# State input of an S5 and gated-GLU kernel: the last 64 features of re and im as half-row products beside those of gate and up

## The chip, the core and the metric

The kernel runs on one core of a Trainium2 chip. The metric is device time in microseconds of one execution. Clocks are granted to TensorE by a throttle; the profile gives the granted clock (here 0.997 of full speed over the span).

## What is computed

Cut to what matters, for x of 2048 tokens by D = 448 features, 448 states and F = 1792:

```
xn = layernorm(x)
Bu = xn @ B_bar^T             # complex: re and im, 448 states each
h[t] = Lam_bar * h[t-1] + Bu[t]     # scan over 2048 tokens, per state
s  = 2 * real(h @ C^T) + xn * Dskip
g  = silu((sigmoid(xn @ w_gate) * (xn @ w_up)) @ w_down)
out = x + s * g
```

The kernel multiplies with B alone; the factor of B_bar is worked into C. The complex scan is turned into two real ones by rotating re and im with tables of cosine and sine.

## The kernel before, in words

Tokens are cut into four chunks of 512. In a chunk all products have features on the partitions and 512 tokens as columns (`xnT`, the normalized input, transposed). 448 features are three whole tiles of 128 rows and one of 64. Names that the steps below use:

- *Gate and up* (`gu_mm`, L589; 14 feature tiles `ft` per chunk): each is three whole products (L603) and one of 64 rows (L597). The 64-row weights of gate lie in rows 0 to 63 of `wt`, those of up in rows 64 to 127, and row tile 3 of `xnT` holds the last 64 features twice (for chunk 0 the second copy is in a fifth tile of its own), so that the two half-row products use the two halves of the rows of TensorE. An even `ft` ends with its halves and an odd `ft` begins with them, so four halves stand together once in two tiles. ScalarE takes the sigmoid of gate (L616) and copies up (L620); VectorE multiplies them to `hF` (L625), one tile later.
- *State input* (`emit_bu`, L454; sets (chunk, pt)): for pt 0 to 2, re and im of 128 states, four products each (L460), the fourth with 64 rows of zeros; pt 3 is one group of four, with the last 64 states of re and of im side by side. ScalarE copies the result to `bus` (L471, L532). Its twelve or so VectorE pieces (rotate L477 to L484, scan L490, rotate back L504 to L512; for pt 3 L538 to L574, with half exchanges by DMA in between, `swap_halves`) go to a list.
- *The planner* (`fill`, L687): pieces are taken from that list, in order, when a running account of TensorE time against VectorE time has room. `unread` counts sets whose `bus` is still to be read. A new set is taken behind an odd `ft` only if fewer than two are unread (L825).
- *Down and output*: `emit_down` (L638, 14 products a token tile of 128, two readings by ScalarE, the product `g_t` L650 on VectorE) and `emit_y` (L658: six products with `h` of pt 0 to 2 L663, one with `h` of pt 3 L665, four with the diagonal of Dskip L669), then `emit_fin` on VectorE (L676, L678) and the store (L679). The outputs of a chunk come in the next chunk, from `ft` 9 on, once all four `h` of it are placed.
- *Banks*: PSUM's eight banks are two for gate (tag g), two for up (u), and four accumulators (acc) for down and output. The state input takes acc in chunk 0, and g and u later.
- *Order*: each engine runs its instructions in the order of the program. All loads, transposes and stores after the first rows are on SP's queue. B comes in rows (`raw`, L146) and is turned by eight DMA transposes into `bT` (`emit_b`, L273, L279). The columns past 448 are zero. The normalized input of chunks 1 to 3 is turned the same way (L257), when ScalarE or VectorE has written it and its second copy of the last 64 features (`ln_twice`). The input of chunk 2, and C with its turns (L163, L167, factors `ct` L428, L429), are loaded in chunk 0.
- *POOL* makes the tables' mirrored halves (`emit_mirror`, L411), a few small vectors and the carries of the scan.

Of the kernel before, what the change touches and what calls it, by code (L numbers as in the profile page):

```python
# [17 lines left out]
D = 448  # L18
F = 1792
P = 128  # L20
TC = 512
# [3 lines left out]
KT = 4  # L25
FT = F // P
DP = KT * P
# [20 lines left out]
def bcast_mid(ap: bass.AP, n: int) -> bass.AP:  # L48
    return ap.unsqueeze(1).to_broadcast((ap.shape[0], n, ap.shape[1]))
# [14 lines left out]
def kernel(  # L64
# [18 lines left out]
    pe, act, dve, pool, sync = nc.tensor, nc.scalar, nc.vector, nc.gpsimd, nc.sync  # L83
# [16 lines left out]
    xnT = [w.tile([P, KT + 1, TC], BF16, name=f"xnT{c}") for c in range(3)]  # L100
# [6 lines left out]
    bT = w.tile([P, KT, NPK], BF16, name="bT")  # L107
# [7 lines left out]
    def load_rows(eng, t, mat, f0, f1):  # L115
        eng.dma_start(out=t[:, 0:3, f0:f1], in_=mat[0:384, f0:f1].rearrange("(kt p) f -> p kt f", p=P))
        eng.dma_start(out=t[0:64, 3, f0:f1], in_=mat[384:448, f0:f1])

    def load_w(eng, f0, f1):
        for t, mat, p0 in ((wg, B_w_gate, 0), (wu, B_w_up, 64)):  # L120
            eng.dma_start(out=t[:, :, f0:f1], in_=mat[0:384, f0:f1].rearrange("(kt p) f -> p kt f", p=P))
            eng.dma_start(out=wt[p0:p0 + 64, f0:f1], in_=mat[384:448, f0:f1])
# [16 lines left out]
    raw = {}  # L139

    def load_x(c):
        if c == 3:
            x_t.append(w.tile([P, TPC, D], BF16, name="x3", tag="tc_re"))
        sync.dma_start(out=x_t[c][:], in_=x_src[:, c * TPC:(c + 1) * TPC, :])

    for nm, mat in (("b_re", A_B_re), ("b_im", A_B_im)):  # L146
        raw[nm] = w.tile([P, KT, DP], BF16, name=nm, tag="raw" + nm[1:])
        dve.memset(raw[nm][:, :, D:DP], 0.0)
        load_rows(sync, raw[nm], mat, 0, D)
    load_w(sync, 512, 1024)  # L150
    load_x(1)

# [116 lines left out]
    def ln_out(j, tp, copy):  # L269
        copy(out=xnT[0][:, :, j * P:(j + 1) * P], in_=tp[:])  # L270


    def emit_b(cc, pt):  # L273
        n = P if pt < 3 else 64
        if cc == 0:
            p0 = pt * P
        else:
            p0 = D if pt == 3 else 512 + pt * P
        sync.dma_start_transpose(out=bT[:, :, p0:p0 + n], in_=raw[("b_re", "b_im")[cc]][0:n, pt, :])  # L279

    def bu_cols(pt, cc):
        if pt == 3:
            return 384, 512
        return (pt * P, (pt + 1) * P) if cc == 0 else (512 + pt * P, 512 + (pt + 1) * P)
# [5 lines left out]
    def col(name, n=KT):  # L290
        return w.tile([P, n], FP32, name=name)
# [19 lines left out]
    def emit_steps():  # L311
        kq, nf, anf = col("kq", 2 * KT), col("nf", 2 * KT), col("anf", 2 * KT)
        tu = col("tu", 2 * KT)
        pool.tensor_copy(out=tu[:, 0:KT], in_=K["turn"][:])
        pool.tensor_single_scalar(out=tu[:, KT:2 * KT], in_=K["theta"][:], scalar=float(TC) / TWO_PI, op=ALU.mult)
        pool.tensor_single_scalar(out=kq[:], in_=tu[:], scalar=MAGIC, op=ALU.add)
        pool.tensor_single_scalar(out=kq[:], in_=kq[:], scalar=-MAGIC, op=ALU.add)
        pool.tensor_tensor(out=nf[:], in0=kq[:], in1=tu[:], op=ALU.subtract)
        dve.tensor_single_scalar(out=anf[:].bitcast(I32), in_=nf[:].bitcast(I32), scalar=0x7FFFFFFF,
                                 op=ALU.bitwise_and)  # L320
        sn, cs = col("sn", 2 * KT), col("cs", 2 * KT)
        act.activation(sn[:], nf[:], ACT.Sin, scale=-SIN_SCALE)
        act.activation(cs[:], anf[:], ACT.Sin, scale=-TWO_PI, bias=hpi[:])
        K.update(sn=sn, cs=cs)
# [118 lines left out]
    unread = [0]  # L443

    def bank(spare, tag, name):
        if spare:
            return ps.tile([P, TC], FP32, name=name, tag="acc", bufs=4)
        return ps.tile([P, TC], FP32, name=name, tag=tag)
# [2 lines left out]
        sync.dma_start(out=o[0:64, :], in_=i[64:128, :])  # L451
        sync.dma_start(out=o[64:128, :], in_=i[0:64, :])

    def emit_bu(c, pt):  # L454
        unread[0] += 1

        def mms(pst, cc):
            lo, hi = bu_cols(pt, cc)
            for kt in range(KT):
                pe.matmul(pst[:], lhsT=bT[:, kt, lo:hi], rhs=xnT[c][:, kt, :],  # L460
                                 start=(kt == 0), stop=(kt == KT - 1))

        rb = K["r"][:, pt:pt + 1].to_broadcast((P, TC))
        mul, add = ALU.mult, ALU.add
# [1 line left out]
        if pt < 3:  # L466
            bus = sp.tile([P, 2, TC], BF16, name="bus", bufs=3)
            for cc in range(2):
                pst = bank(c == 0, ("g", "u")[cc], "bu")
                mms(pst, cc)  # L470
                act.copy(out=bus[:, cc, :], in_=pst[:])  # L471
            cosb = bcast_mid(cosT[:, pt, :], 2)
            sv = spm[:, pt, :, :]

# [51 lines left out]
            for f in (p3, p4, p5):  # L526
                later(0.69, f)
        else:
            pst = bank(c == 0, "g", "bu3")
            mms(pst, 0)  # L530
            bus = sp.tile([P, TC], BF16, name="bus3", tag="bus", bufs=3)
            act.copy(out=bus[:], in_=pst[:])  # L532
            bsw = sp.tile([P, TC], BF16, name="bsw3", bufs=1)
            swap_halves(bsw, bus)

# [50 lines left out]
        if due:  # L586
            due.pop(0)()

    def gu_mm(c, ft, gt, ut, n0=0, n1=TC):  # L589


        f0, f1 = ft * P, (ft + 1) * P
        first = ft % 2 == 1

        def halves():
            for t, p0 in ((gt, 0), (ut, 64)):
                pe.matmul(t[:, n0:n1], lhsT=wt[p0:p0 + 64, f0:f1], rhs=xnT[c][p0:p0 + 64, KT if c == 0 and p0 else 3, n0:n1],  # L597
                          start=first, stop=not first)

        def wholes():  # L600
            for t, wm in ((gt, wg), (ut, wu)):
                for kt in range(3):
                    pe.matmul(t[:, n0:n1], lhsT=wm[:, kt, f0:f1], rhs=xnT[c][:, kt, n0:n1],  # L603
                              start=(not first and kt == 0), stop=(first and kt == 2))

        for part in ((halves, wholes) if first else (wholes, halves)):
            part()

    def emit_gu(c, ft):
        gt, ut = bank(False, "g", "g_ps"), bank(False, "u", "u_ps")  # L610
        gu_mm(c, ft, gt, ut)
        gu_out(c, ft, gt, fp.tile([P, TC], BF16, name="ub"), ut)

    def gu_out(c, ft, gt, ub, ut=None):
        sig = fp.tile([P, TC], BF16, name="sig")
        act.activation(sig[:], gt[:], ACT.Sigmoid)  # L616
        if ut is up_copy:
            up_copy(ft)
        elif ut is not None:
            act.copy(out=ub[:], in_=ut[:])  # L620
        emit_mul()

        def mul():
            h = fp.tile([P, TC], BF16, name="hF", bufs=23)
            dve.tensor_tensor(out=h[:], in0=sig[:], in1=ub[:], op=ALU.mult)  # L625
            hF[c, ft] = h

        due.append(mul)
# [4 lines left out]
    def emit_gate():  # L633
        if due_g:
            due_g.pop(0)()
# [51 lines left out]
    def fill(pe, own):  # L687
        clock[0] += 1
        room[0] = min(room[0] + pe - own, 2.0)
        while pieces and room[0] > 0.0 and clock[0] >= popped[0] + pieces[0][2]:  # L690
            cost, fn, _ = pieces.pop(0)
            popped[0] = clock[0]
            room[0] -= cost
            fn()
# [70 lines left out]
    for pt in range(2, KT):  # L765
        emit_frac(pt)
        emit_sin(pt)
        emit_cos(pt)
    emit_steps()
    for pt in range(KT):  # L770
        emit_neg(pt)
        emit_mirror(pt)
# [36 lines left out]
    at(1, 8, 0.0, lambda: load_x(3))  # L809
    ln_plan(2)  # L810
    ln_plan(3)
    bu_q, out_q = [], []
    room[0] = -2.0
    for c in range(NCH):
        bu_q.extend((c, pt) for pt in range(KT))
        for ft in range(4 if c == 0 else 0, FT):
            emit_gu(c, ft)
            emit_gate()
            for cost, f in beside.pop((c, ft), ()):
                room[0] -= cost  # L820
                f()
            fill(1.62 if c < NCH - 1 or ft < 9 else 2.2, 0.42)
            if ft % 2 == 0:
                continue
            if (4 if c == 0 else 0) < ft < FT - 1 and bu_q and unread[0] < 2:  # L825
                emit_bu(*bu_q.pop(0))
                popped[0] = clock[0]
                fill(1.7, 0.0)
            if c == 0:
                continue  # L830
            if ft < 8:
                emit_down(c - 1, ft // 2)
                fill(2.66, 0.39)
                if ft == 7:
                    out_q.extend((c - 1, j) for j in range(TPC))
            if c == NCH - 1 and ft == FT - 1:
                emit_mul()
            for _ in range(2 if ft == 11 else 1):
                if not (out_q and ft >= 8 and all((out_q[0][0], pt) in hs for pt in range(KT))):
                    break  # L840
                emit_y(*out_q[0])
                emit_fin(*out_q.pop(0))
                fill(1.53, 1.01)
    flush()
    c = NCH - 1
# [38 lines left out]
```

## Time and profile before

| | us |
|---|---|
| three runs, median (lowest to highest) | 197.91 (197.82 to 328.5) |
| the profiled execution | 197.33 |
| its span, first to last instruction | 195.5 |
| TensorE busy (matmul), weight load | 188.8, 90.7 |
| VectorE, ScalarE, POOL busy | 156.8, 111.0, 42.3 |

By stage, each stretch in us from the start of the span:

| stretch | length | TensorE | VectorE | ScalarE |
|---|---|---|---|---|
| start, to 15.5 | 15.5 | 14.10 | 11.06 | 12.63 |
| chunk 0, to 38.0 | 22.5 | 22.24 | 20.86 | 15.83 |
| chunk 1, to 82.7 | 44.7 | 44.30 | 37.67 | 29.35 |
| chunk 2, to 129.3 | 46.6 | 46.17 | 41.18 | 26.20 |
| chunk 3, to 174.7 | 45.4 | 45.19 | 38.07 | 23.09 |
| last outputs, to 195.5 | 20.8 | 16.83 | 7.92 | 3.87 |

How to read the profile: a line of a timeline gives start, duration, engine, source line, operation, output and inputs, shape and count; instructions that follow each other are merged. In brackets stands the idle time before it and what ended that. A group's line gives busy time, mean ns of one, and idle time before it. A matmul's duration is the time from its issue to its modelled end; matmuls that follow each other overlap, so the distance between two starts is what one takes of TensorE's time.

### The profile page before, as it was taken

How to read it: one execution, taken by the hardware profiler on the slowest of the kernel's cores; microseconds unless marked ns; L12 is line 12 of the kernel's file. 1: busy time of each engine (PE TensorE's matmuls, PEld its weight loads, DVE VectorE, ACT ScalarE, POOL GpSimd, SP SyncE). 2: the span in 40 equal slices, each digit the busy share in tenths (PEclk: the TensorE clock that was granted, in tenths of full speed). 3: DMA queues.
4: the chain of work that ended last, by engine and by line, in shares of the span. 5: the costliest groups of instructions: out<-in, count | busy, mean ns of one | idle time of the engine just before them, and what ended most of it. 6: DMA issues, size and time to landing. Idle time of an engine off the chain costs nothing.

```text
span 195.5 us, 3111 instructions
## 1 busy us (share of the span) xinstructions
PE 188.8 (97%) x1069; PEld 90.7 (46%) x1084; DVE 156.8 (80%) x322; ACT 111.0 (57%) x214; POOL 42.3 (22%) x93
## 2 busy tenths in 40 slices
PE   7999999999999999999999999999999999999991
PEld 6874434344444445444444444444444444545561
DVE  4898799948969799999984999999419999994223
ACT  4998666665488856455474586335736644241130
POOL 3535598950302200010321031002100000000000
PEclk9999999999999999999999999999999999999998
DMA  5997994995300302511001001430100010020100
GB/s 153 302 296 140 257 107 86 358 271 100 74 0 15 106 0 64 108 34 27 0 5 29 0 0 38 96 97 0 27 0 3 0 27 2 25 76 23 47 25 23
DMA packets 27593, 14.87 MB, mean 76 GB/s; under 512 B 16309, under 2 KB 27577, under 8 KB 27577
## 3 DMA queue, kind: packets, MB, share of 16 engines
q1 hardware_dynamic: 27568, 14.67, 32.5%
q8 instruction: 8, 0.13, 0.3%
q14 instruction: 9, 0.07, 0.2%
q10 hardware_dynamic: 8, 0.00, 0.0%
HBM read 8.38 MB, written 1.84 MB: 52 GB/s over the span
## 4 chain that ended last, share of the span: by engine, by line
PE 91%; DMA 3%; DVE 2%; issue 1%; ACT 1%; POOL 0%; ACTq 0%; DVEq 0%
PE d_ps L641 22%; PE g_ps L603 20%; PE u_ps L603 18%; PE bu L460 12%; PE y_ps L663 8%; PE g_ps L597 8%; PE y_ps L669 1%; DMA x<-in_A_x_dram 1%; PE y_ps L665 1%; DMA xnT<-xn 1%; DVE stats L207 1%; DVE xnT L270 0%; ACT junk L221 0%; DVE sg L676 0%; POOL sd L234 0%
## 5 line engine op out<-in xcount | busy, mean ns | idle before, releaser
L616 ACT ACTIVATE sig<-g_ps 128x512 bf16<-128x512 f32 x56 | 33.2, 599 | 34.9 <-PE u_ps L597 32.2
L603 PE MATMUL g_ps<-xnT,wg 128*128 128x512 bf16 (+1 forms) x169 | 45.5, 366 | 1.1 <-issue 0.3
L603 PE MATMUL u_ps<-xnT,wu 128*128 128x512 bf16 (+1 forms) x176 | 45.4, 365 | 0.2
L641 PE MATMUL d_ps<-wd,hF 128*128 128x448 bf16 x224 | 45.0, 353 | 0.0
L620 ACT CAST ub<-u_ps 128x512 bf16<-128x512 f32 x52 | 30.3, 583 | 1.7
L641 PEld LDWEIGHTS <-hF 128*128 128x128 bf16 x224 | 21.6, 98 | 20.4
L644 ACT ACTIVATE sigd<-d_ps 128x448 bf16<-128x448 f32 x16 | 8.7, 543 | 33.8 <-PE d_ps L641 33.8
L460 PE MATMUL bu<-xnT,bT 128*128 128x512 bf16 x112 | 26.8, 379 | 0.0
L603 PEld LDWEIGHTS <-wu 128*128 128x128 bf16 x180 | 17.5, 98 | 18.8 <-DMA wu<-in_B_w_up_dram 0.2
L625 DVE TENSOR_TENSOR hF<-sig,ub 128x512 bf16<-128x512 bf16 x56 | 23.4, 420 | 2.3 <-ACT ub L620 2.3
L603 PEld LDWEIGHTS <-wg 128*128 128x128 bf16 x180 | 14.5, 98 | 22.3 <-issue 12.3
L490 DVE TENSOR_TENSOR_SCAN wv<-r_col,st,ta 128x512 bf16<-128x512 f32 x18 | 22.5, 1271 | 0.3
L650 DVE TENSOR_TENSOR g_t<-zb,sigd 128x448 bf16<-128x448 bf16 x16 | 6.2, 390 | 19.1 <-ACT zb L646 19.1
L663 PE MATMUL y_ps<-ct,h 128*128 128x448 bf16 (+1 forms) x102 | 21.0, 342 | 0.0
L597 PE MATMUL g_ps<-xnT,wt 64*128 64x512 bf16 (+1 forms) x60 | 17.2, 367 | 0.0
L597 PE MATMUL u_ps<-xnT,wt 64*128 64x512 bf16 (+1 forms) x60 | 17.2, 367 | 0.0
L460 PEld LDWEIGHTS <-bT 128*128 128x128 bf16 x112 | 11.0, 98 | 13.2
L497 POOL TENSOR_TENSOR tq<-wv,smT 128x2 f32<-128x2 bf16 x9 | 4.1, 450 | 57.6 <-DVE wv L490 57.6
L471 ACT CAST bus<-bu 128x512 bf16<-128x512 f32 x24 | 13.8, 586 | 4.5 <-PE bu L460 4.5
L663 PEld LDWEIGHTS <-h 128*128 128x128 bf16 x102 | 9.7, 98 | 8.3
L207 DVE BATCH_NORM_STATS2 stats<-x 128x6 f32<-128x448 bf16 x14 | 8.6, 617 | 5.8 <-DMA x<-in_A_x_dram 5.8
L676 DVE TENSOR_TENSOR sg<-y_ps,g_t 128x448 bf16<-128x448 f32 (+1 forms) x17 | 10.0, 586 | 0.7 <-PE y_ps L669 0.3
(130 smaller groups left out, 213.6 us busy)
## 6 DMA issues: line engine op xcount, KB each, us to landing
out_dram<-o_t SPq DMA_DIRECT2D x15, 112.0 KB, 1.7
wd<-in_B_w_down_dram SPq DMA_DIRECT2D x1, 1568.0 KB, 7.7
x<-in_A_x_dram SPq DMA_DIRECT2D x3, 448.0 KB, 3.5
wg<-in_B_w_gate_dram SPq DMA_DIRECT2D x2, 384.0 KB, 5.3
wu<-in_B_w_up_dram SPq DMA_DIRECT2D x2, 384.0 KB
wg<-in_B_w_gate_dram SPq DMA_DIRECT2D x1, 576.0 KB, 4.4
wu<-in_B_w_up_dram SPq DMA_DIRECT2D x1, 576.0 KB, 6.6
bsw<-bus SPq DMA_DIRECT2D x8, 64.0 KB, 2.0
```

The costliest lines, as they stand in the source:

```text
L207: dve.bn_stats(out=stats[:], in_=x_t[t // TPC][:, t % TPC, :])
L460: pe.matmul(pst[:], lhsT=bT[:, kt, lo:hi], rhs=xnT[c][:, kt, :], start=(kt == 0), stop=(kt == KT - 1))
L471: act.copy(out=bus[:, cc, :], in_=pst[:])
L490: dve.tensor_tensor_scan(out=T["wv"][:, cc, :], data0=rb, data1=T["ta"][:, cc, :], initial=(0.0 if c == 0 else st[pt][:, cc, :]), op0=mul, ...
L597: pe.matmul(t[:, n0:n1], lhsT=wt[p0:p0 + 64, f0:f1], rhs=xnT[c][p0:p0 + 64, KT if c == 0 and p0 else 3, n0:n1], start=first, stop=not first)
L603: pe.matmul(t[:, n0:n1], lhsT=wm[:, kt, f0:f1], rhs=xnT[c][:, kt, n0:n1], start=(not first and kt == 0), stop=(first and kt == 2))
L616: act.activation(sig[:], gt[:], ACT.Sigmoid)
L620: act.copy(out=ub[:], in_=ut[:])
L625: dve.tensor_tensor(out=h[:], in0=sig[:], in1=ub[:], op=ALU.mult)
L641: pe.matmul(d[:], lhsT=hF[c, ft][:, j * P:(j + 1) * P], rhs=wd[:, ft, :], start=(ft == 0), stop=(ft == FT - 1))
L663: pe.matmul(y[:, d0:d1], lhsT=hs[c, pt][:, cc, sl], rhs=ct[:, 2 * pt + cc, d0:d1], start=(pt == 0 and cc == 0), stop=False)
L676: dve.tensor_tensor(out=sg[:, d0:d1], in0=ys[c, j][:, d0:d1], in1=gs[c, j][:, d0:d1], op=ALU.mult)
```

## The change

For the state input, the last 64 features are taken out of the group of four and become one product of 64 rows for re (rows 0 to 63) and one for im (rows 64 to 127), or re alone for pt 3. They are issued at the start of the group (start=True), right behind the two half-row products of an odd `ft` of gate and up and before its whole products; the three whole products of the state input stay behind that `ft`. So that rows 64 to 127 of `bT` tile 3 hold the last 64 features of im, POOL copies them into the columns past 448 of `b_im` before the transposes; only `b_re` is still filled with zeros there. The banks are always accumulators. Whether a set is taken is decided before the gate and up products of the odd `ft`, and no longer behind them and their `fill`; the allowance of `fill` behind a set goes from 1.7 to 1.5.

```diff
-        dve.memset(raw[nm][:, :, D:DP], 0.0)
         load_rows(sync, raw[nm], mat, 0, D)
+    dve.memset(raw["b_re"][:, :, D:DP], 0.0)
...
+    def emit_b_twice():
+        t = raw["b_im"]
+        pool.tensor_copy(out=t[:, 0:3, D:DP], in_=t[:, 0:3, 384:D])
+        pool.tensor_copy(out=t[0:64, 3, D:DP], in_=t[0:64, 3, 384:D])
...
+    def bu_halves(c, pt):
+        pst = []
+        for cc in range(2 if pt < 3 else 1):
+            p0, (lo, hi) = 64 * cc, bu_cols(pt, cc)
+            t = bank(True, None, "bu")
+            pe.matmul(t[:], lhsT=bT[p0:p0 + 64, 3, lo:hi], rhs=xnT[c][p0:p0 + 64, KT if c == 0 and p0 else 3, :],
+                      start=True, stop=False)
+            pst.append(t)
+        return pst
...
-            for kt in range(KT):
-                pe.matmul(pst[:], lhsT=bT[:, kt, lo:hi], rhs=xnT[c][:, kt, :],
-                                 start=(kt == 0), stop=(kt == KT - 1))
+            for kt in range(3):
+                pe.matmul(pst[:], lhsT=bT[:, kt, lo:hi], rhs=xnT[c][:, kt, :], start=False, stop=(kt == 2))
...
-                pst = bank(c == 0, ("g", "u")[cc], "bu")
-                mms(pst, cc)
-                act.copy(out=bus[:, cc, :], in_=pst[:])
+                mms(pst[cc], cc)
+                act.copy(out=bus[:, cc, :], in_=pst[cc][:])
...
-        for part in ((halves, wholes) if first else (wholes, halves)):
-            part()
+        if not first:
+            wholes()
+        halves()
+        if beside_halves is not None:
+            beside_halves()
+        if first:
+            wholes()
...
     emit_steps()
+    emit_b_twice()
...
         for ft in range(4 if c == 0 else 0, FT):
-            emit_gu(c, ft)
+            bu = None
+            if ft % 2 == 1 and (4 if c == 0 else 0) < ft < FT - 1 and bu_q and unread[0] < 2:
+                bu = bu_q.pop(0)
+                emit_gu(c, ft, lambda: bu_pst.append(bu_halves(*bu)))
+            else:
+                emit_gu(c, ft)
...
-            if (4 if c == 0 else 0) < ft < FT - 1 and bu_q and unread[0] < 2:
-                emit_bu(*bu_q.pop(0))
+            if bu is not None:
+                emit_bu(*bu, bu_pst.pop())
                 popped[0] = clock[0]
-                fill(1.7, 0.0)
+                fill(1.5, 0.0)
```

More of the change, by code (lines that the diff above doesn't have):

```diff
@@ L452, in swap_halves, with emit_bu @@
         sync.dma_start(out=o[64:128, :], in_=i[0:64, :])
-    def emit_bu(c, pt):
+    def bu_halves(c, pt):
[7 more added lines that the diff above has]
+        return pst
+    def emit_bu(c, pt, pst):
         unread[0] += 1
@@ L528, in emit_bu @@
         else:
-            pst = bank(c == 0, "g", "bu3")
-            mms(pst, 0)
+            mms(pst[0], 0)
             bus = sp.tile([P, TC], BF16, name="bus3", tag="bus", bufs=3)
-            act.copy(out=bus[:], in_=pst[:])
+            act.copy(out=bus[:], in_=pst[0][:])
             bsw = sp.tile([P, TC], BF16, name="bsw3", bufs=1)
@@ L587, in emit_mul, with gu_mm @@
             due.pop(0)()
-    def gu_mm(c, ft, gt, ut, n0=0, n1=TC):
+    def gu_mm(c, ft, gt, ut, n0=0, n1=TC, beside_halves=None):
         f0, f1 = ft * P, (ft + 1) * P
@@ L604, in wholes, with emit_gu @@
                               start=(not first and kt == 0), stop=(first and kt == 2))
-        for part in ((halves, wholes) if first else (wholes, halves)):
-            part()
-    def emit_gu(c, ft):
+        if not first:
[5 more added lines that the diff above has]
+            wholes()
+    def emit_gu(c, ft, beside_halves=None):
         gt, ut = bank(False, "g", "g_ps"), bank(False, "u", "u_ps")
-        gu_mm(c, ft, gt, ut)
+        gu_mm(c, ft, gt, ut, beside_halves=beside_halves)
         gu_out(c, ft, gt, fp.tile([P, TC], BF16, name="ub"), ut)
@@ L811 @@
     ln_plan(3)
-    bu_q, out_q = [], []
+    bu_q, out_q, bu_pst = [], [], []
     room[0] = -2.0
```

## The prediction

> **What bounds the kernel now.** I read the page's busy shares and chain of waits, then the groups by line, then the timeline of TensorE around one of the steps that change, and last the timelines of VectorE and ScalarE where a step moves.
>
> ```profile
> PE 188.8 (97%) x1069; PEld 90.7 (46%) x1084; DVE 156.8 (80%) x322; ACT 111.0 (57%) x214; POOL 42.3 (22%) x93
> PE 91%; DMA 3%; DVE 2%; issue 1%; ACT 1%; POOL 0%; ACTq 0%; DVEq 0%
> L460 PE MATMUL bu<-xnT,bT 128*128 128x512 bf16 x112 | 26.8, 379 | 0.0
> ```
>
> TensorE is busy 97% of the span and is 91% of the chain; the state input (`bu`) never waits (idle 0.0). So a TensorE instruction taken away is time taken away, as long as nothing that TensorE waits for becomes late. The 379 ns of one instruction is no price: they overlap. The price is the distance between starts:
>
> ```profile
> 16.40 0.81 PE L603 MATMUL u_ps<-xnT,wu 128*128 128x512 bf16 x3
> 17.14 0.39 PE L597 MATMUL g_ps<-xnT,wt 64*128 64x512 bf16 x1
> 17.14 0.39 PE L597 MATMUL u_ps<-xnT,wt 64*128 64x512 bf16 x1
> 17.37 0.38 PE L597 MATMUL g_ps<-xnT,wt 64*128 64x512 bf16 x1
> 17.37 0.38 PE L597 MATMUL u_ps<-xnT,wt 64*128 64x512 bf16 x1
> 17.68 0.82 PE L603 MATMUL g_ps<-xnT,wg 128*128 128x512 bf16 x3
> 18.34 0.81 PE L603 MATMUL u_ps<-xnT,wu 128*128 128x512 bf16 x3
> 18.98 1.89 PE L460 MATMUL bu<-xnT,bT 128*128 128x512 bf16 x8
> 20.71 0.59 PE L603 MATMUL g_ps<-xnT,wg 128*128 128x512 bf16 x2
> ```
>
> Eight state products take 20.71 - 18.98 = 1.73 us, 0.216 each. A half-row product of gate and one of up start together, and the next pair 0.223 later (0.22 to 0.23 by the rounded rows): two for the price of one. Going in costs 0.09 (16.40 + 3 x 0.216 = 17.05, not 17.14), coming out 0.09 (17.37 + 0.22 = 17.59, not 17.68).
>
> **The change, part by part.**
>
> *Products.* For pt 0 to 2, two whole products of 0.216 become one pair of halves of 0.223: 0.209 saved, for 4 chunks x 3 = 12 sets: **-2.51 us**. The pair joins a section that exists, so the 0.09 in and out aren't paid again. For pt 3, one whole becomes a half with no partner: 4 x (0.223 - 0.216) = +0.03. All of it lies on TensorE's path.
>
> The Trainium skill, "TensorEngine Tiling (Array Packing)", section Performance Considerations, speaks against a gain: tiling makes TensorE faster but not the emptying of PSUM, which may then bound. If it held here the 2.51 would be lost whole. The rows say otherwise for this kernel: ScalarE, which empties these banks, is busy 57%.
>
> *Slots.* Whether a set is taken is now decided before the gate and up products of its slot, when fewer of the earlier set's VectorE pieces have been placed. By the order of the built program seven sets move one odd feature tile later or more: (chunk, pt) (0,3) from behind tile 11 of chunk 0 to tile 1 of chunk 1; (1,0) from 1 to 3, (1,1) from 7 to 9, (1,2) from 9 to 11 of chunk 1; (2,1), (2,2), (2,3) by two tiles each. TensorE's work is the same, so moving costs only through lateness. Two places matter.
>
> *First place, gain: the end of chunk 2.*
>
> ```profile
> 126.81 2.44 DMA xnT<-xn
> 128.75 0.36 PE L669 MATMUL y_ps<-diag,xnT 128*128 128x128 bf16 x4
> 129.30 0.82 PE L603 MATMUL g_ps<-xnT,wg 128*128 128x512 bf16 x3 [0.19 <-DMA xnT<-xn]
> ```
>
> Chunk 3 starts late because its transposed input lands at 129.25. The last diagonal product starts at 128.92, and elsewhere the next product follows 0.03 later, so 0.35 is lost. The transposes are issued after the norm at tile 10. Set (2,3), 3 x 0.216 + 0.22 = 0.87, now lies between tile 10 and chunk 3, so TensorE comes 0.87 later relative to the transposes: **-0.35**. Its two swap transfers also leave SP's queue ahead of the transposes; they had been issued by 119.1, before the norm was ready, so that is worth nothing. Bounds: 0 to -0.35; I take -0.35, as 0.87 covers it twice.
>
> *Second place, loss: the first output of chunk 0.* It needs `h` of pt 3, whose pieces now stand further back on VectorE.
>
> ```profile
> 44.50 0.63 DVE L207 BATCH_NORM_STATS2 stats<-x 128x6 f32<-128x448 bf16 x1 [3.12 <-DMA x<-in_A_x_dram]
> 60.48 1.23 DVE L550 TENSOR_TENSOR_SCAN wv<-r_col,ta 128x512 bf16<-128x512 f32 x1
> 67.21 0.42 DVE L574 TENSOR_TENSOR h<-tcs,td 128x512 bf16<-128x512 bf16 x1
> 71.04 0.35 PE L665 MATMUL y_ps<-ct,h 128*128 128x448 bf16 x1
> ```
>
> Now `h` ends at 67.63, needed at 71.04. VectorE waits at 44.50 for the load of chunk 2, which is not moved, so I count from there. Newly between 44.50 and the scan (steps from start to start): three pieces of earlier sets (0.72 + 0.61 + 0.60), two `hF` (0.67), one `g_t` (0.30), three `ct` (1.80), two small vectors (0.29): 5.0. VectorE idles 1.55 before `ct` at 55.63, because ScalarE's factor comes late; the new work ahead of it fills that. So the scan ends at 61.6 + 5.0 - 1.55 = 65.1. Then the swap through SP: in chunk 3 its reader waits from the scan's end at 173.66 to 176.35, 2.7. So the reader starts at 67.8, `h` ends 0.9 later, at 68.7. TensorE wants it at 71.04, less set (1,2), now behind it (1.73), less five savings (1.05): 68.3. **+0.45** on the path. Bounds: 0 (VectorE 0.45 earlier) and +2.0 (the idle 1.55 not filled). I take 0.45: `ct` is reached at 56.05 by the count, its factor was ready at 55.6.
>
> *Waits of the new pairs.* Six whole products stand behind each, so a late operand or bank stops TensorE. Tightest: set (0,0) at 17.59 needs two `acc` banks whose sigmoids end by
>
> ```profile
> 15.07 2.06 ACT L616 ACTIVATE sig<-g_ps 128x512 bf16<-128x512 f32 x4
> ```
>
> 17.13, and the `b_im` transpose, landed at 16.93 by the trace's landing records; set (0,2), at about 27.1 (22.33 + 4.96, a slot's length, + 0.22 - 0.42), needs one landed at 26.7. Both have 0.4 to spare: 0, bounds 0 and +0.4 (if the transposes slip by 0.8). For the later sets I followed the banks through the built order: each was emptied several us earlier, most by ScalarE, some by the output product on VectorE. Gate and up no longer lend banks; they show no idle for it now, so nothing is gained.
>
> *Two copies on POOL, one memset less on VectorE.* The nearest rows are POOL's copies of 128x255 at 0.40, so 0.8 at most for both. The data has landed at 11.2 (7.04 + 4.2); POOL is idle from 11.34 to 13.20 and only the mirror at 10.94 slips to 12.0, its reader starting at 25.3. SP issues the first `b_im` transpose at 12.95, behind that of `b_re`: 0.9 to spare. Nothing on the path; without that cover at most 0.8 on the transposes, of which 0.4 would reach TensorE. The memset (0.17 at 0.96) lay in VectorE's wait for x: 0.
>
> *The two turns of C* are no longer behind the first swap on SP, but their own load lands at 41.4 and they started at 41.49: 0.
>
> *The tail.* `h` of pt 3, chunk 3, ends at 177.23 and is needed at 178.45, 1.2 spare; one `hF` (0.33) now precedes its scan, and VectorE follows TensorE again from 153.3. 0.9 spare: 0.
>
> **Sum:** -2.51 + 0.03 - 0.35 + 0.45 = -2.38. The profiled execution took 197.33 (span 195.5 and 1.8 around it), so 194.95; the median of the three runs is 197.91, 0.58 above. A measured median of **195.5** follows, 1.2% less. About 2% either way is what a measurement of this kernel can tell from no change.
>
> **Rivals.**
>
> *A. The output waits longer (197.1).* If VectorE's 1.55 idle stays, the wait is 2.0 in place of 0.45. For it: ScalarE's factor waits for a transposed C whose last piece landed at 54.7, unmoved by any speed. Against: 2.0 us of VectorE's work moved ahead of that wait.
>
> *B. The halves don't overlap (198.0).* If re and im ran one after the other, a pair would cost 0.43 and save nothing: -0.35 + 0.45. Against: all 52 pairs in the trace start 2 to 5 ns apart, with the same row halves and other banks.
>
> *C. Slower: `h` of pt 3 very late (198 to 202).* The place is the first output of chunk 0; the price is one us for each us of lateness, and it decides from 2.9 of wait (2.51 + 0.35), that is a scan ending after 67.5 in place of 65.1. For it: VectorE is 80% busy, and the swap and a dozen queued pieces follow. Against: it needs 2.4 us that the count from 44.50 doesn't contain.
>
> **How the numbers follow.** The forecast, 194.8 to 196.4 (wait 0 to 1.2): 0.70. A, to 197.7: 0.14. B: 0.05. C: 0.07, 0.03 of it above 201.9. A gain past what the sum holds: 0.04, 0.03 of it over 2%. Forecast and A make the range, 194.8 to 197.7. Faster by over 2% (below 194.0): 0.03; slower by over 2% (above 201.9): 0.03; within: 0.94.
>
> **What would show it.** Right: `bu` with 12 x 6 + 4 x 3 whole and 28 half products, three pairs 0.22 apart in a section; no DMA wait before chunk 3; VectorE's scan of pt 3 near 65 and an idle of TensorE near 68 to 69 of about 0.5 before L665's successor. Wrong: pairs 0.43 apart (B), an idle of 2 us there (A) or 3 (C), or idle ahead of the first product of a new pair, which would be a bank or a transpose that I called early.

## The result and the profile after

The changed kernel takes 194.61 us in the median of four runs (194.35 to 194.86). The kernel before, run beside it, takes 197.87 (197.70 to 197.91, and one slow run of 328.5 that the ratio leaves out). The ratio is 0.9838, with a 95% interval of 0.9816 to 0.986. In a second measurement it was 194.48 against 197.44: 0.9852 (0.9839 to 0.9866). So the change brings 1.5 to 1.6%. The prediction said 195.5, with 194.8 as its lower end: the sign and the main mechanism were right, the gain was larger than forecast, and the range was too high by 0.2 us.

The profiled execution took 194.83 (span 193.1), against 197.33 (195.5) before. First the busy shares of the page, then the share of the span by engine on the chain that ended last, then the state input's groups (out<-in, shape, count | busy us, mean ns of one | idle before them), all of the changed kernel:

```profile
PE 186.9 (97%) x1084; PEld 88.8 (46%) x1084; DVE 157.2 (81%) x321; ACT 111.7 (58%) x214; POOL 45.1 (23%) x95
...
PE 90%; DMA 3%; ACT 2%; DVE 2%; SPq 1%; issue 1%; ACTq 0%; DVEq 0%
```

```profile
L477 PE MATMUL bu<-xnT,bT 128*128 128x512 bf16 x84 | 20.7, 379 | 0.0
L466 PE MATMUL bu<-xnT,bT 64*128 64x512 bf16 x28 | 6.1, 376 | 0.0
```

There are 84 whole and 28 half products, neither with idle time before it. TensorE is still busy 97% of a span that is 2.5 shorter (195.53 to 193.06). Its timeline around one set of the changed kernel (start, duration, engine, line, output and inputs, shape, count):

```profile
27.15 0.39 PE L611 MATMUL g_ps<-xnT,wt 64*128 64x512 bf16 x1
27.15 0.39 PE L611 MATMUL u_ps<-xnT,wt 64*128 64x512 bf16 x1
27.38 0.38 PE L611 MATMUL g_ps<-xnT,wt 64*128 64x512 bf16 x1
27.38 0.38 PE L611 MATMUL u_ps<-xnT,wt 64*128 64x512 bf16 x1
27.59 0.38 PE L466 MATMUL bu<-xnT,bT 64*128 64x512 bf16 x2
27.91 0.82 PE L617 MATMUL g_ps<-xnT,wg 128*128 128x512 bf16 x3
28.56 0.81 PE L617 MATMUL u_ps<-xnT,wu 128*128 128x512 bf16 x3
29.21 1.03 PE L477 MATMUL bu<-xnT,bT 128*128 128x512 bf16 x4
```

The two half products of the set are one entry ("x2", 0.38 together). The first begins 0.216 after the first of the pair of gate and up, by the raw starts (0.212 after the second), and the way out to 27.91 takes 0.31, as it did without them.

To place the rest I use one measure for all kernels below. The *steady part* runs from the start of the first 512-wide product of gate (`ft` 4, chunk 0) to the start of the last matmul. From it I take off the distances between starts that are longer than elsewhere: between the last diagonal product (the one with the diagonal of Dskip) of a chunk's outputs and the next product of gate (0.028 elsewhere), which is the *wait for the turned input*, and before the product with `h` of pt 3 (0.189 elsewhere), which is the *wait for h*. The *start stall* is the same ahead of the first 512-wide product (0.109 elsewhere). What is left of the steady part is products.

| kernel (one profile each) | start stall | input waits, chunk 2 + 3 | wait for h | steady | products alone | ratio of times to before (95%) |
|---|---|---|---|---|---|---|
| before | 0.00 | 0.28 + 0.35 | 0 | 175.59 | 174.97 | |
| changed | 0.39 | 0 | 0.20 | 172.57 | 172.37 | 0.984 (0.982 to 0.986) |
| changed, measured again | 0.31 | 0 | 0.21 | 172.59 | 172.37 | 0.985 (0.984 to 0.987) |
| banks alone | 0.00 | 0.10 + 0.25 | 0 | 175.31 | 174.97 | 1.000 (0.998 to 1.003) |
| slots alone | 0.00 | 0 | 0 | 174.97 | 174.97 | 0.997 (0.996 to 0.998) |
| halves at old slots | 0.09 | 0.45 + 0.43 | 0 | 173.25 | 172.37 | 0.987 (0.985 to 0.988) |
| before, with copies | 0.00 | 0.58 + 0 | 0 | 175.54 | 174.96 | 1.002 (1.001 to 1.004) |
| before, three times the copies | 0.32 | 0.76 + 0.27 | 0 | 175.98 | 174.96 | 1.003 (1.001 to 1.005) |
| copies on VectorE | 0.00 | 0 | 0.21 | 172.59 | 172.38 | 0.985 (0.983 to 0.986) |
| copies on VectorE, mixed slots | 0.00 | 0 | 0 | 172.36 | 172.36 | 0.984 (0.983 to 0.986) |
| both on rows 0 to 63 | 0.08 | 0 | 0 | 174.92 | 174.92 | 0.996 (0.995 to 0.998) |
| halves in their own section | 0.00 | 0 | 0 | 175.76 | 175.76 | 1.000 (0.998 to 1.002) |
| C's factors a tile earlier | 0.00 | 0 | 0.75 | 173.12 | 172.38 | 0.988 (0.985 to 0.991) |

The column "products alone" has four levels and agrees to 0.02 within each. So the few waits named explain the whole difference between the steady parts of any two of these profiles, and 174.97 - 172.37 = 2.60 is what the half products are worth. The start lies outside: besides the stall, the first 512-wide product comes 7.5 to 7.8 us after the first product of gate, and that one starts anywhere from 8.0 to 8.8, in kernels with and without the half products. So a time can move by 0.8 for a reason that these experiments don't touch.

### The profile page after: what moved, and what is told of

Same layout as the page of the kernel before. It is cut to its first block, busy times and chain, and to the rows that moved or that the text cites. A ratio compares the mean times of both kernels' runs of the same rounds, so it can differ in the third digit from the quotient of the medians.

```text
span 193.1 us, 3130 instructions
## 1 busy us (share of the span) xinstructions
PE 186.9 (97%) x1084; PEld 88.8 (46%) x1084; DVE 157.2 (81%) x321; ACT 111.7 (58%) x214; POOL 45.1 (23%) x95
## 4 chain that ended last, share of the span: by engine, by line
PE 90%; DMA 3%; ACT 2%; DVE 2%; SPq 1%; issue 1%; ACTq 0%; DVEq 0%
PE d_ps L660 22%; PE g_ps L617 19%; PE u_ps L617 18%; PE bu L477 9%; PE y_ps L682 9%; PE g_ps L611 7%; DMA wu<-in_B_w_up_dram 3%; PE bu L466 2%; PE y_ps L684 2%; PE y_ps L688 2%; ACT L635 0%; ACT cosT L406 0%; DVE xnT L270 0%; DVE frac L395 0%; ACT spm L403 0%
## 5 line engine op out<-in xcount | busy, mean ns | idle before, releaser
L617 PE MATMUL g_ps<-xnT,wg 128*128 128x512 bf16 (+1 forms) x180 | 46.4, 367 | 0.3 <-ACT sig L635 0.2
L617 PE MATMUL u_ps<-xnT,wu 128*128 128x512 bf16 (+1 forms) x180 | 46.1, 365 | 0.1
L477 PE MATMUL bu<-xnT,bT 128*128 128x512 bf16 x84 | 20.7, 379 | 0.0
L512 POOL TENSOR_TENSOR tq<-wv,smT 128x2 f32<-128x2 bf16 x9 | 5.1, 569 | 56.2 <-DVE wv L505 56.2
L477 PEld LDWEIGHTS <-bT 128*128 128x128 bf16 x84 | 8.2, 98 | 9.9
```

## The experiments

Two theories stood against each other after the result. Mine: the gain is 12 pairs, plus the waits for the turned input that the new slots remove, less a wait for h and a start that the POOL copies delay. The rival: the start was late by chance, the slots bring nothing, and the rest of the gain has another cause.

**Halves at the old slots, and slots alone.** These two, with the kernels before and changed, cross the two parts of the change.

```diff
-            if ft % 2 == 1 and (4 if c == 0 else 0) < ft < FT - 1 and bu_q and unread[0] < 2:
+            if (c, ft) in {(0, 5), (0, 7), (0, 9), (0, 11), (1, 1), (1, 7), (1, 9), (2, 1), ...}:
```

> The changed kernel with its sets at the slots of the kernel before and the allowance 1.7: half products, banks and POOL copies stay. Theory: 12 pairs save 2.64, the copies cost 0.4, the waits for the turned input before chunks 2 and 3 are back with about 0.28 and 0.35, no wait in the first output of chunk 0: 2.25 faster than before, 0.4 slower than the changed kernel. Rival (the transposed input lands at a fixed time, so that TensorE, now earlier, waits longer for it): the two waits grow to 1.5 to 2.9 and half of the saving or more is gone.

Measured: 194.58 (before 197.34), 2.8 faster by the medians where 2.25 was expected: the POOL copies cost 0.09 in this profile, not 0.4. The steady part is 2.34 shorter, and both waits are back:

```profile
80.97 0.36 PE L688 MATMUL y_ps<-diag,xnT 128*128 128x128 bf16 x4
81.62 0.59 PE L617 MATMUL g_ps<-xnT,wg 128*128 128x512 bf16 x2 [0.29 <-DMA xnT<-xn]
...
126.99 0.36 PE L688 MATMUL y_ps<-diag,xnT 128*128 128x128 bf16 x4
127.61 0.61 PE L617 MATMUL g_ps<-xnT,wg 128*128 128x512 bf16 x2 [0.27 <-DMA xnT<-xn]
```

That the waits grow with an earlier TensorE (the rival's 1.5 to 2.9) is refuted: they are 0.45 and 0.43. The transposes follow ScalarE's norm, which follows TensorE: counted from the first 512-wide product, the norm of chunk 2 ends at 58.36 (59.66 in the kernel before), and the first transpose is issued at 58.38 (59.68).

The other half: the kernel before with the table of the changed kernel and its allowance of 1.5.

> The kernel before (whole products in groups of four, its own banks, no copies), with its sets at the slots of the changed kernel and the allowance 1.5: VectorE's order is that of the changed kernel. Theory: both waits for the turned input go (0.28 before chunk 2, 0.35 before chunk 3), the first output of chunk 0 waits 0.2 to 0.5 for `h` of pt 3: 0.1 to 0.45 faster than before. Rival (the slots cost as much as they bring, or more, and the gain beyond the pairs has another cause): same or slower.

Measured: 196.82 against 197.34, 0.5 faster, just past the 0.45 expected. Both waits are gone, as before chunk 2 in this timeline, where 0.19 lies between the merged diagonal products and the next (three at 0.056, one at 0.028):

```profile
82.88 0.36 PE L669 MATMUL y_ps<-diag,xnT 128*128 128x128 bf16 x4
83.07 0.81 PE L603 MATMUL g_ps<-xnT,wg 128*128 128x512 bf16 x3
```

The wait for h that I had expected did not come. `h` of pt 3 ends at 69.86 and TensorE's product with it starts at 69.92, just in time: counted from the first 512-wide product, TensorE comes there 1.1 later than it could in the changed kernel, and `h` only 0.9 later. For the turned input, all eight profiles with a set behind tile 11 of chunks 1 and 2 have no wait. The five with the old slots have 0.35 to 1.02 in sum, another amount in each execution.

**Both on rows 0 to 63.** The im half takes `p0 = 0` too.

```diff
-            p0, (lo, hi) = 64 * cc, bu_cols(pt, cc)
+            p0, (lo, hi) = 0, bu_cols(pt, cc)
```

> The changed kernel with the im half of each state set on rows 0 to 63 too (from b_im's own columns), so that re and im use the same half of the rows. Theory (the gain is that the two halves of the rows work at the same time): the second product starts 0.21 to 0.22 after the first in place of 0.003, 12 x 0.216 = 2.6 slower than the changed kernel. Rival (the gain is that products of 64 rows are shorter, or that fewer rows of zeros are fed): start distances below 0.15 or within 0.5 us of the changed kernel.

Measured: 196.80, against 194.48 for the changed kernel beside it; products 2.55 longer than there. The second product starts 0.215 after the first in place of 0.003:

```profile
27.45 0.59 PE L466 MATMUL bu<-xnT,bT 64*128 64x512 bf16 x2
27.97 0.82 PE L617 MATMUL g_ps<-xnT,wg 128*128 128x512 bf16 x3
```

0.59 for the two in place of 0.38, and 0.52 in place of 0.32 to the next product. A product of 64 rows takes as long as one of 128 (0.215 against 0.216), so 2.55 of the 2.60 is the overlap of the two row halves.

**Halves in a section of their own.** The half products are issued in front of the state input's own whole products, not beside those of gate and up.

```diff
-                emit_gu(c, ft, lambda: bu_pst.append(bu_halves(*bu)))
+                emit_gu(c, ft)
...
-                emit_bu(*bu, bu_pst.pop())
+                emit_bu(*bu, bu_halves(*bu))
```

> The changed kernel with the half products of the state input issued behind the whole products of the odd tile, ahead of the state input's own whole products, in place of beside the halves of gate and up; slots, banks, copies as changed. Theory (a pair costs 0.212 only because it joins a section that exists; each going in and coming out costs 0.095 and 0.09 more): 16 sections of their own cost 16 x 0.185 = 3.0, so the steady part is 172.6 + 3.0 = 175.6, as long as before the change. Rival (two halves for one whole are a gain wherever they stand): steady part below 173.5.

Measured: 197.68 (before 197.54), steady 175.76. The whole gain is gone: 3.39 for 16 sections is 0.21 each, where 0.185 was expected. In its timeline three whole products of `u_ps` take 0.74 to the pair where 0.65 is usual, and the pair 0.32 to the next product:

```profile
28.55 0.81 PE L617 MATMUL u_ps<-xnT,wu 128*128 128x512 bf16 x3
29.29 0.39 PE L466 MATMUL bu<-xnT,bT 64*128 64x512 bf16 x2
29.61 0.60 PE L477 MATMUL bu<-xnT,bT 128*128 128x512 bf16 x2
```

**Banks alone.** The kernel before with `bank(True, None, ...)` in all chunks.

> The kernel before with accumulator banks for the state input in all four chunks, as in the change; everything else as before. Theory (the banks were never waited for): no idle of TensorE for a bank, steady part 175.3 to 175.9 with the waits for the turned input as they fall, time within 0.2 of before. Rival (gate and up had waited for the banks that they lent): 0.3 us or more faster.

Measured: 197.28 against 197.54 (ratio 1.000, 0.998 to 1.003), products 174.97 as in the kernel before. So the banks change nothing in TensorE's products; the times alone could hide 0.5 us either way.

**The POOL copies.** VectorE makes four `frac` instructions at the start (fractions of a turn, from which ScalarE makes the tables of cosine and sine), the third at about the time when POOL copies. Four kernels bear on it. First the changed kernel with the copies on VectorE:

```diff
-        pool.tensor_copy(out=t[:, 0:3, D:DP], in_=t[:, 0:3, 384:D])
-        pool.tensor_copy(out=t[0:64, 3, D:DP], in_=t[0:64, 3, 384:D])
+        dve.tensor_copy(out=t[:, 0:3, D:DP], in_=t[:, 0:3, 384:D])
+        dve.tensor_copy(out=t[0:64, 3, D:DP], in_=t[0:64, 3, 384:D])
```

> The changed kernel with the two copies of b_im's last 64 columns on VectorE, behind the last of its `frac` work, in place of POOL; all else as changed. Theory (a POOL copy beside VectorE's `frac` makes that `frac` take 0.89 in place of 0.48 us, ScalarE's tables and first sigmoid come 0.4 later, TensorE stands 0.23 before its first 512-wide product): the `frac` takes 0.48 again, the idle before the first 512-wide product goes, time 0.35 to 0.4 below the changed kernel, near 194.2. Rival (the start was late by chance, by a load that landed late): time as the changed kernel, 194.6 +- 0.2, and the `frac` long or short as it falls.

Measured: 194.26, `frac` 0.47, start stall 0. The times alone don't show it (ratio 0.985, against 0.984 and 0.985 for the changed kernel): that the stall goes is read from the profile. Then the kernel before with the same copies into a tile `scr` that nobody reads:

> The kernel before with the two POOL copies added at the same place, into a tile that nobody reads. Theory: the third `frac` takes 0.89, the first sigmoid comes 0.4 later, and since its bank was free only 0.04 before TensorE came for it, 0.37 of that is lost: 0.35 to 0.4 slower than before. Rival (POOL does not slow VectorE): within 0.1 of before.

Measured: 197.73 against 197.34, ratio 1.0021 (1.0005 to 1.0037). Its profile, of an execution that took 197.23, has `frac` at 0.47 and no stall. So the theory as I wrote it missed in that execution: POOL's first copy of b_im began at 10.48 (11.15 in the changed kernel), and POOL was through in time. That execution was the fastest of eight; their median is 0.39 above before, as the theory had it, but no profile shows why. The changed kernel run again was to test that:

> The changed kernel once more, beside the others of this batch. Both theories: the last matmul starts 172.55 to 172.6 us after the first 512-wide product, as before. Theory (a POOL copy slows VectorE's `frac` when the load of b_im lands so late that they meet): the `frac` is 0.47 if the mirror copy behind the two copies starts before 11.0, and up to 0.9 if it starts later. Rival (chance): no such relation.

Measured: 194.48; mirror copy at 11.18, `frac` 0.81, stall 0.31. And the certain collision, six copies in place of two (`for _ in range(3)`):

> The kernel before with the two POOL copies made three times into a tile that nobody reads, so that POOL is certain to copy while VectorE makes the third and the fourth `frac` (about 11.2 to 12.5). Theory: at least one of the two takes 0.8 to 0.95 in place of 0.48, ScalarE idles 0.3 to 0.8 more before its tables, the first 512-wide product starts 0.35 to 0.8 later than the u product before it allows; time 0.35 to 0.8 above before. Rival (POOL and VectorE don't disturb each other): both 0.48, within 0.1 of before.

Measured: 198.10 against 197.44. VectorE and POOL of that kernel:

```profile
11.14 0.51 DVE L396 SCALAR_TENSOR_TENSOR frac<-iota_f,turn,whole 128x256 f32<-128x256 f32 x1
...
11.96 0.80 DVE L396 SCALAR_TENSOR_TENSOR frac<-iota_f,turn,whole 128x256 f32<-128x256 f32 x1
```

```profile
11.13 0.23 POOL L278 COPY scr<-b_im 64x64 bf16<-64x64 bf16 x1
11.31 0.54 POOL L277 COPY scr<-b_im 128x192 bf16<-128x192 bf16 x1
11.80 0.34 POOL L278 COPY scr<-b_im 64x64 bf16<-64x64 bf16 x1
12.08 0.40 POOL L419 COPY cosT<-cosT 128x255 bf16<-128x255 bf16 x1
```

The fourth `frac` waits for POOL (0.80 in place of 0.48); in the third, POOL's copy waits for VectorE (0.54 in place of 0.34). The stall is 0.32, a little under the 0.35 expected; the rest of this kernel's loss in its profile is that it drew 1.02 of waits for the turned input. The changed kernel itself, VectorE and POOL:

```profile
11.39 0.89 DVE L395 SCALAR_TENSOR_TENSOR frac<-iota_f,turn,whole 128x256 f32<-128x256 f32 x1
```

```profile
11.15 0.34 POOL L276 COPY b_im<-b_im 128x192 bf16<-128x192 bf16 x1 [1.49 <-DMA b_im<-in_A_B_im_dram]
11.43 0.23 POOL L277 COPY b_im<-b_im 64x64 bf16<-64x64 bf16 x1
11.61 0.40 POOL L418 COPY cosT<-cosT 128x255 bf16<-128x255 bf16 x1
```

and where it ends, on ScalarE, which idles 0.76 before its table (0.18 in the kernel before), and on TensorE, where the product of gate would follow three of up at 15.55 + 3 x 0.11 = 15.88 and comes at 16.27:

```profile
12.31 0.42 ACT L403 ACTIVATE spm<-frac 128x256 bf16<-128x256 f32 x1 [0.76 <-DVE frac L395]
...
15.63 1.58 ACT L635 ACTIVATE sig<-g_ps 128x512 bf16<-128x512 f32 x3
```

```profile
15.55 0.49 PE L617 MATMUL u_ps<-xnT,wu 128*128 128x256 bf16 x3
16.27 0.81 PE L617 MATMUL g_ps<-xnT,wg 128*128 128x512 bf16 x3 [0.23 <-ACT sig L635]
```

What counts for the third `frac` is how far POOL's last copy of the row, the mirror's, reaches past its start. Six profiles:

| kernel | POOL past the start of `frac` | `frac` | start stall |
|---|---|---|---|
| before, with copies | 11.36 - 11.19 = 0.17 | 0.47 | 0.00 |
| copies on VectorE | 11.31 - 11.13 = 0.18 | 0.47 | 0.00 |
| both on rows 0 to 63 | 11.44 - 11.13 = 0.31 | 0.58 | 0.08 |
| halves at old slots | 11.50 - 11.18 = 0.32 | 0.59 | 0.09 |
| changed, measured again | 11.58 - 11.04 = 0.54 | 0.81 | 0.31 |
| changed | 12.01 - 11.39 = 0.62 | 0.89 | 0.39 |

Above 0.2 `frac` takes its 0.48 and the overlap less 0.2, and the stall is that excess less 0.02. In the other seven profiles the overlap is 0.09 to 0.23 and this `frac` takes 0.48 to 0.51. So the collision is real, and chance decides only how much of it there is, by when b_im lands and when VectorE comes to `frac`. The rows fit a lock rather than a sharing of bandwidth: where `frac` takes 0.89, the three POOL copies beside it keep their 0.34, 0.23 and 0.40. The Trainium skill, "SBUF — State Buffer", section "Who interferes with whom", has the rule: a VectorE instruction with two inputs in SBUF contends with a GpSimd (POOL) instruction that reads SBUF, the contention is an exclusive lock, and the order of issue decides which of them waits. `frac` has two such inputs, and the rows agree, in both orders.

**Where the wait for h comes from.** First the wait itself. The six products ahead of the one with `h` of pt 3 take 71.04 - 69.90 = 1.14 in the kernel before; in the changed kernel it is 68.95 - 67.62 = 1.33:

```profile
69.90 1.30 PE L663 MATMUL y_ps<-ct,h 128*128 128x448 bf16 x6
71.04 0.35 PE L665 MATMUL y_ps<-ct,h 128*128 128x448 bf16 x1
```

```profile
67.62 1.30 PE L682 MATMUL y_ps<-ct,h 128*128 128x448 bf16 x6
68.95 0.36 PE L684 MATMUL y_ps<-ct,h 128*128 128x448 bf16 x1
```

Two kernels look for its cause. The factors of C for i 4 to 6 are issued a tile earlier on ScalarE:

```diff
-        at(1, 4 + i // 2, 0.68, lambda i=i: emit_c(i))
+        at(1, 4 + i // 2 - (i > 3), 0.0, lambda i=i: c_ready.update({i: emit_c(i)}))
+        at(1, 4 + i // 2, 0.68, lambda i=i: c_ready.pop(i)())
```

> The changed kernel with ScalarE's share of the last three factors of C (c_tmp of i 4, 5, 6) issued one feature tile earlier; VectorE's share keeps its place. Theory (VectorE's idle of 1.29 and 0.18 before those factors makes h of pt 3 of chunk 0 late, and h alone holds TensorE in the first output): that idle goes, the scan of pt 3 ends about 1.2 earlier, the wait of 0.2 in the first output goes, steady part 172.38. Rival (the swap by DMA or the pieces ahead of the scan set the end): h within 0.3 us of where it was, the wait stays at 0.2.

Measured: 195.06, and the wait grew to 0.75. VectorE no longer waits for a factor, but for `zb`, which ScalarE now makes behind the factors; the chain stays as it was, only later:

```profile
60.89 0.39 DVE L671 TENSOR_TENSOR g_t<-zb,sigd 128x448 bf16<-128x448 bf16 x1 [0.84 <-ACT zb L667]
...
64.52 1.23 DVE L566 TENSOR_TENSOR_SCAN wv<-r_col,ta 128x512 bf16<-128x512 f32 x1
...
68.44 0.43 DVE L577 TENSOR_TENSOR td<-wsw,spm 128x512 bf16<-128x512 bf16 x1 [1.25 <-DMA wsw<-wv]
```

The scan starts 0.55 later after the first 512-wide product than in the changed kernel (48.36 against 47.81), and TensorE waits 0.55 more: one for one. So h does hold TensorE, but my way to make it earlier failed. The other way gives (0,3), (1,0) and (1,1) back their old slots, so that fewer pieces stand ahead of the scan of pt 3 (table of slots, copies on VectorE):

> The changed kernel with the copies of b_im on VectorE and a mixed table of slots: (0,3), (1,0), (1,1) where the kernel before had them, all others as changed, so that `h` of pt 3 of chunk 0 is early and the sets (1,2) and (2,3) still stand ahead of chunks 2 and 3. Theory (the 0.2 before the diagonal products of the first output of chunk 0 is the lateness of h of pt 3, and the turned input waits only where no set stands between): no idle of TensorE at either place, 0.2 faster than with the copies on VectorE alone, steady part 172.38. Rival (the wait moves to another reader, or the input waits return): steady part 172.6 or more.

Measured: 194.21, steady 172.36, no wait anywhere. The scan starts 47.41 after the first 512-wide product (47.81 in the changed kernel) and `h` ends 0.4 earlier; the last factor is no longer waited for. By its profile this is the best kernel, 0.2 below the copies on VectorE alone and 0.5 to 0.6 (wait and stall) below the changed kernel; the intervals of the timed ratios overlap, so the times alone don't separate the three.

## Why the prediction was right and wrong

*Products (-2.48 with pt 3's): right, 2.60 measured.* The price of a pair by distance between starts held; only its size was off. A pair of the state input comes 0.216 after the pair of gate and up, not 0.223, so each saves 0.216 (12 x 0.216 = 2.59), and the single half of pt 3 costs nothing more than the whole that it replaces. Rival B (halves one after the other) is refuted: the two start 3 to 4 ns apart, and they follow each other only where both were put on the same rows.

*End of chunk 2 (-0.35): right in kind, one place missed.* The same wait stood before chunk 2. I had not seen it, because the trace's idle time counts from the modelled end of the product before. Of the kernel before:

```profile
82.26 0.36 PE L669 MATMUL y_ps<-diag,xnT 128*128 128x128 bf16 x4
82.73 0.81 PE L603 MATMUL g_ps<-xnT,wg 128*128 128x512 bf16 x3
```

and of the changed kernel:

```profile
81.69 0.36 PE L688 MATMUL y_ps<-diag,xnT 128*128 128x128 bf16 x4
81.89 0.81 PE L617 MATMUL g_ps<-xnT,wg 128*128 128x512 bf16 x3
```

0.47 against 0.20 from the first diagonal product, with no bracket in either: another 0.28 that set (1,2) covers.

*First output of chunk 0 (+0.45): right place, 0.20 measured, by another path.* The step counted VectorE's work from the load of chunk 2 to the scan. What sets the scan is ScalarE's last factor of C. In the three profiles with the changed kernel's order of these steps (changed, measured again, copies on VectorE) the load comes 26.8, 28.4 and 28.1 us after the first 512-wide product, and yet the last `ct` starts 46.3 after it in all three, behind an idle of 0.13 to 0.19, and the scan 47.81. The first of them:

```profile
43.06 0.63 DVE L207 BATCH_NORM_STATS2 stats<-x 128x6 f32<-128x448 bf16 x1 [2.73 <-DMA x<-in_A_x_dram]
...
60.48 0.69 DVE L435 SCALAR_TENSOR_TENSOR ct<-tc_re,cr,c_tmp 128x448 bf16<-128x448 bf16 x1 [1.29 <-ACT c_tmp L434]
...
62.57 0.69 DVE L435 SCALAR_TENSOR_TENSOR ct<-tc_re,cr,c_tmp 128x448 bf16<-128x448 bf16 x1 [0.18 <-ACT c_tmp L434]
...
64.08 1.23 DVE L564 TENSOR_TENSOR_SCAN wv<-r_col,ta 128x512 bf16<-128x512 f32 x1
...
68.45 0.44 DVE L588 TENSOR_TENSOR h<-tcs,td 128x512 bf16<-128x512 bf16 x1
```

The step said that the load "is not moved" and that the new work fills the idle. The idle of 1.55 before the first `ct` is filled, but 1.29 opens before the fifth, and the load came 2.0 earlier than in the kernel before (0.3 in the second measurement), counted from the first 512-wide product. That the 20.6 counted from the load to the end of the scan comes out exactly in the second measurement (44.26 to 64.87) is luck: in the first it is 22.2.

*POOL copies (0): wrong.* The step found "nothing on the path". It asked who reads what POOL makes, and not what VectorE does at that time. The copies cost TensorE 0 to 0.39, by the execution.

*Banks, operands of the new pairs (0): right.* No idle stands before any of the 28 half products, and ScalarE, busy 58%, empties their banks in time.

*The sum and its conversion: the sum held by cancelling, the conversion failed.* For the profiled execution the forecast was 194.95, and 194.83 was measured. By the terms measured: -2.60 products, -0.63 input waits, +0.20 wait for h, +0.39 start stall, and +0.13 because a weight load landed later (the first `u_ps` at 8.68 in place of 8.55) make -2.51; the measured -2.50. The gain was forecast too low by 0.65 in the products, the input waits and h, and the cost too low by 0.52 in the start. What put the answer outside the range is the step "0.58 above. A measured median of 195.5 follows". In three further measurements the kernel before had medians of 197.34, 197.44 and 197.54 (18 to 20 runs each), so its profiled 197.33 was ordinary and the two runs behind the 197.91 were high. The changed kernel beside them shows no such excess: 194.61, against 194.48 in the second measurement. Without the 0.58 the forecast is 194.95 and the range begins at 194.2, below what was measured. An excess can indeed fail to carry over: the waits for the turned input vary from execution to execution (0.35 to 1.02 in the five profiles with the old slots), and these are what the change removes. Whether those two runs had such long waits isn't known, as only their spans are; so why they were high stays open.

## What to carry to other kernels

Two half-row products beside each other cost one, but only inside a section that already exists; a section of their own costs 0.21 us here and eats the gain of 0.216. Read waits as distances between starts against the usual distance, not as the idle that a view prints, and a wait that varies between executions is no constant to add to a forecast. Before a small copy is put on POOL, look at what VectorE does at that time, not only at who reads the copy.

## What the runs showed of the hardware that was not expected

`frac`, a VectorE instruction with two SBUF inputs, that comes while POOL copies is held up by all of POOL's copies that follow each other in the profile, not only by the one that was running: it ends 0.28 after the end of the last (three in a row in the changed kernel: `frac` came at 11.39, during the first, and ended at 12.28 = 12.01 - 0.2 + 0.48). Whether the 0.2 is time that `frac` needs before it reads, or a late end in POOL's records, no run here tells. In the other order POOL's copy waits: 0.54 in place of 0.34, seen once.
